# A 47-point DFT folded by the parity of its index, inside a fused FFT and feed-forward kernel

## The chip, the cores and the metric

The kernel runs on one core of a Trainium2 chip. Five engines matter: TensorE (PE in the profile; its weight loads are PEld), VectorE (DVE), ScalarE (ACT), GpSimd (POOL) and SyncE (SP), which issues most of the DMAs. The metric is the time of one execution on the device in microseconds (us), the median of the runs.

## The reference

The real part of a 2-D Fourier transform over 3008 positions and 256 features, for 8 batches, followed by a two-layer feed-forward block with a piecewise activation. Everything is float32.

```
X = np.fft.fft(x, axis=1)          # x: (8, 3008, 256)
X = np.fft.fft(X, axis=2)
x = X.real.reshape(B * S, D)
h = x @ w_in                       # w_in: (256, 2048)
g = np.where(h >= 1, h, np.where(h <= -1, 0.0, (h + 1) ** 2 / 4))
return g @ w_out                   # w_out: (2048, 256)
```

## The kernel before, in words

The 3008 positions are written as 64 x 47 (two coprime factors), so that their transform is a 47-point DFT followed by a 64-point DFT without twiddle factors. The transform over the 256 features is folded into `w_in` when the program starts (`fold_w_in`). Since the input is real, position s and position -s share most of the work: the kernel works on 24 of the 47 frequencies and on the sum and the difference of two halves.

**The transform of a batch** is a list of pieces (`fft_pieces`, L321). Stage 1 (`stage1`, L258) is the 47-point DFT. The host has already laid out x as two summands for each value; `fold_x` (L126) lets GpSimd add them: `y = t[:, 0] + t[:, 1]` (L131), 96 partitions by 512 elements, where the 96 partitions are two groups of 47 points and a padding row each. Then four float32 matmuls per tile (L270) take 128 columns of y as the stationary operand, and move the 96 columns of the constant `bm`, which holds two blocks of cosine and sine. Eight tiles (`XC`) make a batch: 32 matmuls of 94 used rows by 96 columns. Tile 0 also has the Nyquist feature: GpSimd subtracts 96 x 64 elements (L137, tile `yd`), and one small matmul (L275) transforms it. ScalarE copies the results out of PSUM into z, four copies of 64 x 192 a tile (L280) and two of 64 x 24 for the Nyquist feature (L283). `nyquist` (L285) and six pieces of stage 2 (`stage2`, L299, the 64-point DFT, matmul L309 with 128 columns moving) end the transform; ScalarE and VectorE split its result into a high and a low part, `pqh` and `pql`. In batch 0 the even tiles are not added on GpSimd: TensorE accumulates the two summands instead, which takes two matmuls for one.

**The feed-forward block** runs in units: one unit is one of 16 slices of 128 hidden features on one of three column chunks (482, 512 and 512 wide) of a batch, 48 units to a batch; batch 0 goes over its chunks twice with 8 slices each. `gemm1` (L350) makes two PSUM banks `uv` with six matmuls (L359). VectorE makes `us` (L362) and two halves of `h` (L364, L365); ScalarE computes the activation's square (L372, L373); VectorE finishes h (L374, two tiles of SBUF in, one out); ScalarE rounds it to `gh` (L375); GpSimd makes the rest `gl = h - gh` in two halves (L378). `gemm2` (L381) comes four units later (`LAG`): twelve matmuls (L402) that accumulate into four PSUM banks `acc`. The `uv` banks rotate over three buffers, `h` and `a` over three, `gh` and `gl` over four.

**The order.** Each engine runs its own instructions in a fixed order. A scheduler decides that order from the program text, except on TensorE for the first matmul of each piece of a later batch (`pinned`, L316) and for the start. The pieces of the next batch's transform are spread over the 48 units of the current batch (for batch 1: over units 25 to 47 of batch 0). The x tiles of the next batch come by SyncE into buffers tagged `xt`, four of them, which the weights' raw data shared while they were converted during batch 0; y rotates over three buffers. The loads of the first four x tiles are written at the first unit of the batch before (`FIRST_LOAD`, unit 21, for batch 1), the rest follow piece by piece.

Of the kernel before, what the change touches and what calls it, by code (L numbers as in the profile page):

```python
# [31 lines left out]
C_ORDER = [*range(1, 8), 0, *range(8, NC)]  # L32
WIDTH = [7 * NA + 34, CH, CH]

G_ORDER = np.arange(P).reshape(XC, GPC, 2, 2).transpose(0, 3, 1, 2).reshape(-1)


def _constants():
    a, b, k = (np.arange(n) for n in (NA, NBB, D))
    bm = np.zeros((P, 96))  # L40
    ang = 2 * np.pi * (np.outer(b, C_ORDER) % NBB) / NBB
    for t in range(2):
        o = t * 2 * NC
        bm[o : o + NBB, o : o + NC] = np.cos(ang)
        bm[o : o + NBB, o + NC : o + 2 * NC] = np.sin(ang)
# [22 lines left out]
START = "p0 p1 c0 p2 p3 c1 f0 p4 p5 p6 p7 d0 p8 p9 p10 c4 c5"  # L70
# [39 lines left out]
def fft_ffn_kernel(ctx: ExitStack, tc: tile.TileContext, x, cst, w_in, w_out, out):  # L110
# [7 lines left out]
    xt, yt, zt, nyb, pq = {}, {}, {}, {}, {}  # L118

    def load_x(b, q):  # L120
        tag, bufs = ("xt", 4) if b or q < 4 else ("gl", 4) if q < 7 else ("o", 2)
        t = sb.tile([96, 2, CH], F32, tag=tag, name=f"x_{b}_{q}", bufs=bufs)
        nc.sync.dma_start(t, x[b, q])
        xt[b, q] = t

    def fold_x(b, q):  # L126

        t = xt.pop((b, q))
        if b or q % 2:
            y = sb.tile([96, CH], F32, tag="y", name=f"y_{b}_{q}", bufs=3)  # L130
            nc.gpsimd.tensor_tensor(y, t[:, 0], t[:, 1], op=ALU.add)  # L131
            yt[b, q] = [y]
        else:
            yt[b, q] = [t[:, 0], t[:, 1]]
        if q == 0:
            y = sb.tile([96, NA], F32, tag="yd", name=f"yd_{b}", bufs=1)
            nc.gpsimd.tensor_tensor(y, t[:, 0, :NA], t[:, 1, :NA], op=ALU.subtract)  # L137
            yt[b, "d"] = y
# [39 lines left out]
    def load_w(n):  # L178
        if n >= len(jobs):
            return  # L180
        kind, *at = jobs[n]
# [8 lines left out]
        raws[n] = raw  # L190

    def convert_w(n):

        raw = raws.pop(n)
        low, high = raw[:, :, 0], raw[:, :, 1]
        if n in CV:
            tag, bufs = CV[n]
            t = sb.tile([P, 2, CH], U32, tag=tag, name=f"cv_{n}", bufs=bufs)
            man, exp = t[:, 0], t[:, 1]
            lowf, shifted = low.bitcast(F32), exp  # L200
        else:
# [54 lines left out]
        nc.scalar.activation(delta[:, f4 * 4 : f4 * 4 + 4], pt, AF.Copy)  # L256

    def stage1(b, q):  # L258
        for p in range(q, min(q + 2, XC)):
# [4 lines left out]
        z, y = zt[b], yt[b, q]
        bank = fft_bank(b, f"s1_{b}_{q}")
        pt = bank[:, : GPC * 96].rearrange("p (i n) -> p i n", i=GPC)
        for i in range(GPC):
            for j, part in enumerate(y):
                lhs = part[:, i * P : (i + 1) * P]
                mm = nc.tensor.matmul(pt[:, i], lhs, bm[:96, :], start=(j == 0), stop=(j == len(y) - 1))  # L270
                if i == 0:
                    pinned(b, mm)
        if q == 0:
            pd = bank[:NA, GPC * 96 : GPC * 96 + 2 * NC]
            nc.tensor.matmul(pd, yt[b, "d"], bm[:96, : 2 * NC], start=True, stop=True)  # L275
        for h in range(2):
            for m in range(2):
                src = pt[h * NA : (h + 1) * NA].rearrange("p i (t m c) -> p m c (i t)", t=2, m=2)[:, m]
                dst = z[m * NA : (m + 1) * NA, :, (2 * q + h) * 8 : (2 * q + h + 1) * 8]
                nc.scalar.activation(dst, src, AF.Copy)  # L280
        if q == 0:
            for m in range(2):
                nc.scalar.activation(z[m * NA : (m + 1) * NA, :, P], pd[:, m * NC : (m + 1) * NC], AF.Copy)  # L283
# [248 lines left out]
```

## Time and profile before

| What | Value |
|---|---|
| Median of 3 runs | 1766.23 us (1762.65 to 1767.64) |
| The profiled execution: its span, first to last instruction | 1761.8 us |
| The profiled execution: its own time beside the span | not given; the median of the runs lies 4.4 us above the span |
| Granted TensorE clock, mean | 0.997 |
| Stage-1 and Nyquist matmuls of stage 1 (L270, L275), instructions | 544 and 16 |
| GpSimd: gl (L378), y (L131), yd (L137), instructions | 765, 60, 8 |

The span is cut into engines' busy time; a busy share near 100% says that an engine has no rest, not that it runs at its peak, since matmuls overlap. What an engine waits for is listed with the engine and line that ended the wait. A float32 matmul (L270, L275, L287, L309, L246) shows as two instructions, a matmul of type float32r (L359, L402) as one.

### The profile page before, as it was taken

The page shows a single profiled execution, that of the slowest core. Times are in us where ns is not written, and L with a number is a line of the kernel's source. Part 1 is how long each engine was busy: PE and PEld are TensorE (multiplying, and loading weights), DVE is VectorE, ACT ScalarE, POOL GpSimd, SP SyncE. Part 2 cuts the span into 40 slices and gives each one's busy share as a digit, 9 for nine tenths or more (in the row PEclk, how much of TensorE's full clock was granted, in tenths as well). Part 3 has the DMA queues.
Part 4 walks back from the last instruction along what each step waited for, and adds up shares of the span by engine and source line. Part 5 has one row for each costly group of instructions (what it writes and reads, how often), then busy time and mean ns, then how long its engine had stood idle before and what let it go on. Part 6 is the DMA issues. An engine that isn't in the chain of part 4 may idle for free.

```text
span 1761.8 us, 21916 instructions
## 1 busy us (share of the span) xinstructions
PE 1734.5 (98%) x7982; PEld 1419.5 (81%) x7982; DVE 1428.0 (81%) x1745; ACT 1356.3 (77%) x1601; POOL 1203.4 (68%) x838
## 2 busy tenths in 40 slices
PE   9889999999999999999999999999999999999998
PEld 6766888888888888888888888888888888888777
DVE  6998788888887888778887788878888778888887
ACT  5777877877777877877778877788778787777776
POOL 1545966876668766787667876677676766667775
PEclk9999999999999999999999999999999999999999
DMA  7013331011010100111001100011000001000000
GB/s 230 12 65 102 101 107 57 28 50 42 1 51 28 53 30 1 51 50 31 30 10 51 50 28 24 23 39 51 26 24 34 1 23 35 8 25 6 17 24 24
DMA packets 29963, 72.51 MB, mean 41 GB/s; under 512 B 2976, under 2 KB 8224, under 8 KB 29856
## 3 DMA queue, kind: packets, MB, share of 16 engines
q1 hardware_dynamic: 29568, 70.08, 12.3%
q8 instruction: 62, 1.02, 0.3%
q10 hardware_dynamic: 288, 1.05, 0.2%
q14 instruction: 45, 0.37, 0.1%
HBM read 43.31 MB, written 27.81 MB: 40 GB/s over the span
## 4 chain that ended last, share of the span: by engine, by line
PE 73%; ACT 7%; POOL 5%; DVE 3%; issue 3%; ACTq 0%; POOLq 0%; DVEq 0%
PE acc L402 45%; PE uv L359 23%; POOL gl L378 5%; DVE h L374 3%; ACT gh L375 2%; PE s L270 2%; ACT a L373 2%; PE s L309 2%; ACT a L372 2%; ACT z L280 0%; ACT o L413 0%; DVE h L364 0%; DVE h L365 0%; POOL y L131 0%; DVE o L410 0%
## 5 line engine op out<-in xcount | busy, mean ns | idle before, releaser
L378 POOL TENSOR_TENSOR gl<-h,gh 128x512 fp32r<-128x512 f32 (+1 forms) x765 | 1096.7, 1456 | 510.6 <-ACT gh L375 478.0
L374 DVE SCALAR_TENSOR_TENSOR h<-a,h 128x1024 f32<-128x1024 f32 (+1 forms) x385 | 578.1, 1502 | 223.8 <-ACT a L373 222.2
L375 ACT ACTIVATE gh<-h 128x1024 fp32r<-128x1024 f32 (+1 forms) x385 | 400.6, 1041 | 346.1 <-DVE h L374 300.0
L402 PE MATMUL acc<-gl,woh 128*128 128x512 f32 (+1 forms) x1536 | 604.5, 394 | 9.2 <-POOL gl L378 9.2
L402 PE MATMUL acc<-gh,woh 128*128 128x512 f32 (+1 forms) x1536 | 608.0, 396 | 5.6 <-ACT gh L375 3.1
L402 PE MATMUL acc<-gh,wol 128*128 128x512 f32 (+1 forms) x1536 | 595.7, 388 | 0.0
L372 ACT ACTIVATE a<-h,biases 128x1024 f32<-128x1024 f32 (+1 forms) x385 | 431.8, 1122 | 9.7 <-DVE h L365 7.7
L373 ACT ACTIVATE a<-a 128x1024 f32<-128x1024 f32 (+1 forms) x385 | 398.7, 1036 | 7.1
L402 PEld LDWEIGHTS acc<-gl,woh 128*128 128x128 f32 x1536 | 288.6, 188 | 76.7 <-POOL gl L378 16.9
L402 PEld LDWEIGHTS acc<-gh,woh 128*128 128x128 f32 x1536 | 289.3, 188 | 66.3 <-ACT gh L375 4.9
L402 PEld LDWEIGHTS acc<-gh,wol 128*128 128x128 f32 x1536 | 289.5, 188 | 59.4
L364 DVE TENSOR_TENSOR h<-us,uv 128x512 f32<-128x512 f32 (+1 forms) x384 | 259.2, 675 | 67.2 <-POOL gl L378 26.0
L359 PE MATMUL uv<-pqh,wh 128*128 128x512 f32 (+1 forms) x768 | 303.8, 396 | 3.8 <-DVE us L362 3.3
L359 PE MATMUL uv<-pql,wh 128*128 128x512 f32 (+1 forms) x768 | 301.5, 393 | 0.0
L359 PE MATMUL uv<-pqh,wl 128*128 128x512 f32 (+1 forms) x768 | 299.1, 389 | 0.0
L362 DVE SCALAR_TENSOR_TENSOR us<-nyb,delta,uv 128x512 f32<-128x512 f32 (+1 forms) x384 | 278.4, 725 | 17.3 <-PE uv L359 16.9
L365 DVE TENSOR_TENSOR h<-us,uv 128x512 f32<-128x512 f32 (+1 forms) x384 | 255.9, 666 | 0.0
L359 PEld LDWEIGHTS uv<-pqh,wh 128*128 128x128 f32 x768 | 144.2, 188 | 42.7 <-DVE us L362 8.2
L359 PEld LDWEIGHTS uv<-pql,wh 128*128 128x128 f32 x768 | 144.5, 188 | 31.9
L359 PEld LDWEIGHTS uv<-pqh,wl 128*128 128x128 f32 x768 | 144.3, 188 | 30.3 <-issue 0.2
L131 POOL TENSOR_TENSOR y<-x 96x512 f32<-96x512 f32 x60 | 106.4, 1774 | 19.9 <-DMA x<-in_x_dram 8.1
L280 ACT ACTIVATE z<-s 64x192 f32<-64x192 f32 x256 | 86.8, 339 | 7.2 <-PE s L275 2.2
(54 smaller groups left out, 543.1 us busy)
## 6 DMA issues: line engine op xcount, KB each, us to landing
x<-in_x_dram SPq DMA_DIRECT2D x64, 384.0 KB, 3.4
out_dram<-o SPq DMA_DIRECT2D x30, 512.0 KB, 2.8
out_dram<-o SPq DMA_DIRECT2D x16, 482.0 KB, 3.2
nyb<-nyr SPq DMA_DIRECT2D x24, 256.0 KB, 3.2
raw<-in_moe_w_out_dram SPq DMA_DIRECT2D x8, 512.0 KB, 10.8
raw<-in_moe_w_in_dram SPq DMA_DIRECT2D x6, 512.0 KB, 4.5
part<-o SPq DMA_DIRECT2D x4, 512.0 KB, 3.3
o<-part SPq DMA_DIRECT2D x4, 512.0 KB
```

The source lines that it names most:

```text
L131: nc.gpsimd.tensor_tensor(y, t[:, 0], t[:, 1], op=ALU.add)
L280: nc.scalar.activation(dst, src, AF.Copy)
L359: nc.tensor.matmul(t[:, :n], w[m][:, cols], r[:, m, :n], start=(j == 0), stop=(j == 2))
L362: nc.vector.scalar_tensor_tensor(us, nyb[b, k][:, :n], delta[:, f : f + 1], uv[0], op0=ALU.mult, op1=ALU.add)
L364: nc.vector.tensor_tensor(h[:, 0], us, uv[1], op=ALU.subtract)
L365: nc.vector.tensor_tensor(h[:, 1], us, uv[1], op=ALU.add)
L372: nc.scalar.activation(a[:, sl], h[:, sl], AF.Relu, bias=half, scale=0.5)
L373: nc.scalar.activation(a[:, sl], a[:, sl], AF.Square)
L374: nc.vector.scalar_tensor_tensor(h[:, sl], a[:, sl], 1.0, h[:, sl], op0=ALU.min, op1=ALU.max)
L375: nc.scalar.activation(gh[:, sl], h[:, sl], AF.Copy)
L378: eng.tensor_tensor(gl[:, sg], h[:, sg], gh[:, sg].bitcast(F32), op=ALU.subtract)
L402: nc.tensor.matmul(acc[:, :n], w[:, f, wc], g[:, sg], start=(first and j == 0), stop=(last and j == 2))
```

## The change

The points b and 47 - b of the 47-point DFT have the same cosine and opposite sines. The new code adds and subtracts them first, so that 24 rows instead of 47 stand for one group, once for the cosine part and once for the sine part. A row block of 24 (`HB`) fits five times into 120 rows (`KR`, five groups, `GJ`), where two groups of 47 fitted into 94.

- The host lays out x as [120 partitions, 2, 4, 128]: four summands for each value (the two of before, each at b and at 47 - b). Six full tiles and a half one (7, `XC`) make a batch. The Nyquist feature sits in a slot of the half tile, and its own matmul and copies are gone.
- `fold_x` adds summand 1 to 0 and 3 to 2, in place, in one GpSimd instruction of 120 x 4 x 128 (for the half tile 96 x 2 x 128, and a subtraction of 24 x 2 x 64).
- `mirror_x`, for batches 1 to 7, makes the sum and the difference of the two results, in place, in two GpSimd instructions of 120 x 2 x 128 (120 x 128 for the half tile).
- `stage1` has 26 matmuls a batch, 120 rows by 120 columns: four a full tile, two for the half one. In batch 0 there is no mirror: 26 matmuls of 240 columns, two accumulated for each result.
- ScalarE copies 64 x 240 elements, four times a full tile, and 64 x 120 and 64 x 96, twice each, for the half one.
- x rotates over five buffers of `xt`; the three y buffers and `yd` are gone. The first four x loads of a batch are written four units (`LOAD_AHEAD`) ahead of the first unit in which that batch's transform may run, its first fold two units and its first mirror one unit ahead. `stage1` folds up to two tiles ahead and mirrors one ahead.
- The constants loaded first grow from 226 to 490 columns.

The core of the diff:

```diff
-XC = 8
-GPC = 4
+HB = 24
+GJ = 5
+KR = GJ * HB
+XC = 7
...
-        t = xt.pop((b, q))
-        if b or q % 2:
-            y = sb.tile([96, CH], F32, tag="y", name=f"y_{b}_{q}", bufs=3)
-            nc.gpsimd.tensor_tensor(y, t[:, 0], t[:, 1], op=ALU.add)
-            yt[b, q] = [y]
...
+        pair = t.rearrange("p r (k two) x -> p two (r k) x", two=2)
+        n = KR if q < XC - 1 else KR - HB
+        nc.gpsimd.tensor_tensor(pair[:n, 0], pair[:n, 0], pair[:n, 1], op=ALU.add)
+        if n < KR:
+            nyq = pair[n:, :, :, :NA]
+            nc.gpsimd.tensor_tensor(nyq[:, 0], nyq[:, 0], nyq[:, 1], op=ALU.subtract)
+
+    def mirror_x(b, q):
...
+            nc.gpsimd.tensor_tensor(t[:, :, 1], t[:, :, 0], t[:, :, 2], op=ALU.add)
+            nc.gpsimd.tensor_tensor(t[:, :, 3], t[:, :, 0], t[:, :, 2], op=ALU.subtract)
...
-        for p in range(q, min(q + 2, XC)):
-            if (b, p) in xt and (b, p) not in yt:
+        for p in range(q, min(q + 3, XC)):
+            if (b, p) in xt:
                 fold_x(b, p)
+                if p < q + 2:
+                    mirror_x(b, p)
...
-        for i in range(GPC):
-            for j, part in enumerate(y):
-                lhs = part[:, i * P : (i + 1) * P]
-                mm = nc.tensor.matmul(pt[:, i], lhs, bm[:96, :], start=(j == 0), stop=(j == len(y) - 1))
...
+        for r in range(n):
+            if b:
+                for m in range(2):
+                    mm = nc.tensor.matmul(pt[:, m, r], t[:, r, 2 * m + 1], bm[:KR, m], start=True, stop=True)
...
+            else:
+                for k in range(2):
+                    nc.tensor.matmul(
+                        pt[:, :, r], t[:, r, 2 * k], bm[:KR, : 2 + k : 1 + k], start=(k == 0), stop=(k == 1)
+                    )
...
-            if r == (0 if b else FIRST_LOAD) and b + 1 < NB:
-                for q in range(4):
-                    load_x(b + 1, q)
+            for nb in range(1, NB):
+                ahead = (per * (nb - 1) if nb > 1 else FIRST_DFT) - i
+                if ahead == LOAD_AHEAD:
+                    for q in range(4):
+                        load_x(nb, q)
+                elif ahead == 2:
+                    fold_x(nb, 0)
+                elif ahead == 1:
+                    mirror_x(nb, 0)
```

What this does to the order is seen best on GpSimd, around unit 103. In the names the first number behind `gl` is the unit, the first two behind `x` and `y` are batch and tile. Before:

```order
L378 TENSOR_TENSOR gl_102_4492<-h_102_4487,gh_102_4491 128x482 x2
L378 TENSOR_TENSOR gl_103_4539<-h_103_4534,gh_103_4538 128x482 x2
L131 TENSOR_TENSOR y_3_6_4876<-x_3_6_4510 96x512
L378 TENSOR_TENSOR gl_104_4573<-h_104_4568,gh_104_4572 128x482 x2
L378 TENSOR_TENSOR gl_105_4607<-h_105_4602,gh_105_4606 128x482 x2
L378 TENSOR_TENSOR gl_106_4654<-h_106_4649,gh_106_4653 128x482 x2
L378 TENSOR_TENSOR gl_107_4688<-h_107_4683,gh_107_4687 128x482 x2
L131 TENSOR_TENSOR y_3_7_5031<-x_3_7_4625 96x512
```

and the same place in the changed program:

```order
L405 TENSOR_TENSOR gl_102_4433<-h_102_4428,gh_102_4432 128x482 x2
L148 TENSOR_TENSOR x_4_0_5844<-x_4_0_5844 120x4x128
L158 TENSOR_TENSOR x_4_0_5844<-x_4_0_5844 120x2x128
L159 TENSOR_TENSOR x_4_0_5844<-x_4_0_5844 120x2x128
L405 TENSOR_TENSOR gl_103_4467<-h_103_4462,gh_103_4466 128x482 x2
L405 TENSOR_TENSOR gl_104_4515<-h_104_4510,gh_104_4514 128x482 x2
L405 TENSOR_TENSOR gl_105_4549<-h_105_4544,gh_105_4548 128x482 x2
L405 TENSOR_TENSOR gl_106_4583<-h_106_4578,gh_106_4582 128x482 x2
L148 TENSOR_TENSOR x_4_1_5846<-x_4_1_5846 120x4x128
L158 TENSOR_TENSOR x_4_1_5846<-x_4_1_5846 120x2x128
L159 TENSOR_TENSOR x_4_1_5846<-x_4_1_5846 120x2x128
L405 TENSOR_TENSOR gl_107_4617<-h_107_4612,gh_107_4616 128x482 x2
```

Where one instruction stood between two units, three now stand together. In a later batch's stretch such bursts stand behind the `gl` of units 95, 98, 102, 106, 109, 113 and 115 (of the 48 units 96 to 143, and so on in each batch); before, the eight y stood behind units 94, 98, 100, 103, 107, 110, 114 and 117.

TensorE meets the first tile of batch 4 in unit 144, long after that. Before:

```order
L359 MATMUL uv_144_1_6069<-pql_3_0_5340,wh1_70 128x482
L270 MATMUL s1_4_0_6094<-cs_66,y_4_0_6087 128x96 x4
L275 MATMUL s1_4_0_6094<-cs_66,yd_4_6089 64x48
L402 MATMUL acc_128_0_5651<-gh_140_5928,woh_73 128x512
L402 MATMUL acc_128_0_5651<-gh_140_5928,wol_74 128x512
```

and now:

```order
L386 MATMUL uv_144_1_6002<-pql_3_0_5168,wh1_70 128x482
L295 MATMUL s1_4_0_6025<-cs_66,x_4_0_5844 128x120 x4
L429 MATMUL acc_128_0_5581<-gh_140_5866,woh_73 128x512
L429 MATMUL acc_128_0_5581<-gh_140_5866,wol_74 128x512
```

The place of the piece is the same; its four matmuls are 120 columns wide, and the Nyquist matmul behind them is gone. Tile 0 of batch 4 is folded and mirrored some 37 units before TensorE reads it.

More of the change, by code (lines that the diff above doesn't have):

```diff
@@ L33, with _slots @@
 WIDTH = [7 * NA + 34, CH, CH]
-G_ORDER = np.arange(P).reshape(XC, GPC, 2, 2).transpose(0, 3, 1, 2).reshape(-1)
+def _slots():
+    table = np.full((XC, 2, 2, GJ), -1)
+    g = np.arange(120).reshape(XC - 1, 2, 2, GJ)
+    table[: XC - 1] = g.transpose(0, 2, 1, 3)
+    table[XC - 1, 0, 1, :4] = np.arange(120, 124)
+    table[XC - 1, 0, 0, :4] = np.arange(124, 128)
+    table[XC - 1, 0, 0, 4] = 0
+    return table
 def _constants():
-    a, b, k = (np.arange(n) for n in (NA, NBB, D))
-    bm = np.zeros((P, 96))
+    a, b, k = (np.arange(n) for n in (NA, HB, D))
+    bm = np.zeros((P, 3, KR))
     ang = 2 * np.pi * (np.outer(b, C_ORDER) % NBB) / NBB
[L42 to L45, printed above, removed]
+    for j in range(GJ):
+        o = slice(j * HB, (j + 1) * HB)
+        bm[o, 0, o] = np.cos(ang)
+        bm[o, 1, o] = np.sin(ang)
+        bm[o, 2, o] = -np.sin(ang)
+    bm = bm.reshape(P, 3 * KR)
     ang = 2 * np.pi * (np.outer(a, a) % NA) / NA
@@ L73 @@
     0: "o2",
-    1: "f1 d1 o3 p11",
-    2: "p12",
-    3: "p13 p14 l8 l9",
+    1: "f1 d1 o3 p10",
+    2: "p11",
+    3: "p12 p13 l8 l9",
     4: "c6",
@@ L92 @@
 }
-FIRST_LOAD, FIRST_DFT = 21, 25
+FIRST_DFT, LOAD_AHEAD = 25, 4
 N_EARLY = 8
@@ L116, in fft_ffn_kernel @@
     ps = ctx.enter_context(tc.tile_pool(name="ps", bufs=1, space=bass.MemoryType.PSUM))
-    xt, yt, zt, nyb, pq = {}, {}, {}, {}, {}
+    xt, zt, nyb, pq = {}, {}, {}, {}
+    folded, mirrored = set(), set()
     def load_x(b, q):
-        tag, bufs = ("xt", 4) if b or q < 4 else ("gl", 4) if q < 7 else ("o", 2)
-        t = sb.tile([96, 2, CH], F32, tag=tag, name=f"x_{b}_{q}", bufs=bufs)
-        nc.sync.dma_start(t, x[b, q])
+        tag, bufs = ("xt", 5) if b or q < 4 else ("gl", 4)
+        n = 2 if q < XC - 1 else 1
+        t = sb.tile([KR, 2, 4, P], F32, tag=tag, name=f"x_{b}_{q}", bufs=bufs)[:, :n]
+        nc.sync.dma_start(t, x[b, q, :, :n])
         xt[b, q] = t
     def fold_x(b, q):
-        t = xt.pop((b, q))
-        if b or q % 2:
-            y = sb.tile([96, CH], F32, tag="y", name=f"y_{b}_{q}", bufs=3)
-            nc.gpsimd.tensor_tensor(y, t[:, 0], t[:, 1], op=ALU.add)
-            yt[b, q] = [y]
[L133 to L138, printed above, removed]
+        t = xt[b, q]
+        if (b, q) in folded:
+            return
+        folded.add((b, q))
+        pair = t.rearrange("p r (k two) x -> p two (r k) x", two=2)
[5 more added lines that the diff above has]
+    def mirror_x(b, q):
+        t = xt[b, q]
+        if b and (b, q) not in mirrored:
+            mirrored.add((b, q))
+            nc.gpsimd.tensor_tensor(t[:, :, 1], t[:, :, 0], t[:, :, 2], op=ALU.add)
+            nc.gpsimd.tensor_tensor(t[:, :, 3], t[:, :, 0], t[:, :, 2], op=ALU.subtract)
     cs = wts.tile([P, _OFF[3]], F32, name="cs")
@@ L142, in fft_ffn_kernel @@
     bm, rm, odd = (cs[:, _OFF[i] : _OFF[i + 1]] for i in range(3))
-    cm = sb.tile([P, _OFF[7] - _OFF[3]], F32, tag="y", name="cm", bufs=3)
+    bm = bm.rearrange("p (m x) -> p m x", m=3)
+    cm = sb.tile([P, _OFF[7] - _OFF[3]], F32, tag="nyb", name="cm", bufs=4)
     mats = [[cm[:, (2 * m + h) * P : (2 * m + h + 1) * P] for h in range(2)] for m in range(2)]
@@ L181, in load_w @@
         kind, *at = jobs[n]
-        raw = sb.tile([P, CH, 2], U32, tag="xt" if n >= N_EARLY else RAW[n], name=f"raw_{n}", bufs=4)
+        raw = sb.tile([P, CH, 2], U32, tag="xt" if n >= N_EARLY else RAW[n], name=f"raw_{n}", bufs=5 if n >= N_EARLY else 4)
         if kind == "in":
@@ L202, in convert_w @@
             if n % 2 == 0:
-                f32s["pair"] = sb.tile([P, 2, CH], U32, tag="xt", name=f"cv_{n}", bufs=4)
+                f32s["pair"] = sb.tile([P, 2, CH], U32, tag="xt", name=f"cv_{n}", bufs=5)
             man, exp = f32s["pair"][:, n % 2], high
@@ L267, in stage1 @@
-        for i in range(GPC):
-            for j, part in enumerate(y):
-                lhs = part[:, i * P : (i + 1) * P]
[L270 to L275, printed above, removed]
+        pt = bank[:, : 2 * n * KR].rearrange("p (m r x) -> p m r x", m=2, r=n)
@@ L276, in stage1 @@
+        for r in range(n):
+            if b:
+                for m in range(2):
+                    mm = nc.tensor.matmul(pt[:, m, r], t[:, r, 2 * m + 1], bm[:KR, m], start=True, stop=True)
+                    if r + m == 0:
+                        pinned(b, mm)
+            else:
[3 more added lines that the diff above has]
+                    )
         for h in range(2):
+            cols = n * GJ
+            first = 20 * q + cols * h
+            if n == 1:
+                cols, first = (4, 120) if h else (5, 124)
@@ L277, in stage1 @@
             for m in range(2):
[L278 to L283, printed above, removed]
+                src = pt[h * NA : (h + 1) * NA, m].rearrange("p r (j c) -> p c (r j)", j=GJ)[:, :, :cols]
@@ L285, in nyquist @@
+                nc.scalar.activation(z[m * NA : (m + 1) * NA, :, first : first + cols], src, AF.Copy)
     def nyquist(b):
@@ L323, in fft_pieces @@
         for q in range(XC):
-            pieces.append((4, lambda q=q: stage1(b, q)))
+            pieces.append((4 if q < XC - 1 else 2, lambda q=q: stage1(b, q)))
         pieces.append((2, lambda: nyquist(b)))
@@ L502 @@
     xs = np.stack([xs[:, n][..., g], xs[:, neg][..., np.where(g == 0, P, D - g)]])
-    xs = xs.reshape(2, NB, NA, NBB, XC, GPC, 2, 2).transpose(1, 4, 6, 3, 0, 5, 7, 2)
-    xp = np.zeros((NB, XC, 2, 2 * NC, 2, GPC, 2, NA), xs.dtype)
-    xp[:, :, :, :NBB] = xs
+    slots = _slots()
+    used = (slots >= 0)[:, :, :, :, None, None]
+    xp = np.zeros((NB, XC, GJ, HB, 2, 4, 2, NA), xs.dtype)
+    for k in range(4):
+        bs = np.arange(HB) if k < 2 else (NBB - np.arange(HB)) % NBB
+        part = np.where(used, xs[k % 2].transpose(0, 3, 2, 1)[:, slots][..., bs, :], 0)
+        if k >= 2:
+            part[..., 0, :] = 0
+        xp[:, :, :, :, :, k] = part.transpose(0, 1, 4, 5, 2, 3, 6)
     arrays = {
-        "x": xp.reshape(NB, XC, 96, 2, CH),
+        "x": xp.reshape(NB, XC, KR, 2, 4, P),
         "cst": _CONST,
```

13 lines of the change are left out of this document (6 added, 7 removed).

## The prediction

> **What bounds the kernel now.** First the head of the page, then the windows view from 205 to 1540 us (first row) and the waits of TensorE in the same stretch (the other two).
>
> ```profile
> span 1761.8 us, 21916 instructions
> PE 1734.5 (98%) x7982; PEld 1419.5 (81%) x7982; DVE 1428.0 (81%) x1745; ACT 1356.3 (77%) x1601; POOL 1203.4 (68%) x838
> ...
> 205.00:1540.00 1335.00, 1334.07 (x6211) 1105.45 (x6212) 1077.07 (x1280) 1045.90 (x1223) 953.54 (x659) 1.00 0.11 35
> ...
> PE s L270 <- ACT z L280: 1.1, 1, 1.1
> PE uv L359 <- DVE h L365: 0.4, 1, 0.4
> ```
>
> For 1335 us TensorE waits 1.5 us in all. A matmul taken away there shortens the kernel; work given to GpSimd (953.5 of 1335 us busy) costs nothing until it makes TensorE wait. Six of the seven later batches' transforms (batches 2 to 7) lie in that stretch, the seventh (batch 1) mostly ahead of it. I work against this execution's span, 1761.8 us; the median of the runs, 1766.2, is 4.4 us above it, and I add that at the end. A measurement of this kernel tells about 0.3% (5.3 us) from no change.
>
> **What TensorE saves.** The timeline of TensorE at three pieces of the transform: stage 1, stage 1 with the Nyquist row, stage 2. Columns are start, length, line, tiles; each f32 matmul shows as two instructions.
>
> ```profile
> 507.47 1.03 PE L270 MATMUL s<-cs,y 96*128 96x96 f32 x8
> 508.28 0.47 PE L402 MATMUL acc<-gh,woh 128*128 128x482 f32 x1
> 508.59 0.38 PE L402 MATMUL acc<-gh,wol 128*128 128x482 f32 x1
> 508.81 0.39 PE L402 MATMUL acc<-gl,woh 128*128 128x482 f32 x1
> ...
> 279.32 1.03 PE L270 MATMUL s<-cs,y 96*128 96x96 f32 x8
> 280.28 0.32 PE L275 MATMUL s<-cs,yd 96*64 96x48 f32 x2
> 280.52 0.51 PE L402 MATMUL acc<-gh,woh 128*128 128x512 f32 x1
> 280.87 0.40 PE L402 MATMUL acc<-gh,wol 128*128 128x512 f32 x1
> 281.10 0.40 PE L402 MATMUL acc<-gl,woh 128*128 128x512 f32 x1
> ...
> 264.38 1.05 PE L309 MATMUL s<-cs,z 128*128 128x128 f32 x8
> 265.18 0.48 PE L359 MATMUL uv<-pqh,wh 128*128 128x512 f32 x1
> 265.50 0.40 PE L359 MATMUL uv<-pqh,wl 128*128 128x512 f32 x1
> 265.73 0.40 PE L359 MATMUL uv<-pql,wh 128*128 128x512 f32 x1
> ```
>
> Lengths overlap, so I count from start to start. Stage 1: from 507.47 to the second matmul behind it, 508.59, is 1.12 us; one GEMM matmul (508.59 to 508.81) is 0.22; the piece costs 0.90 us, 0.112 an instruction. With the Nyquist pair: 1.55 - 0.23 = 1.32. Stage 2, with 128 columns moving and 128 rows: 1.12 - 0.23 = 0.89. So 96 and 128 columns, and 96 and 128 rows, have one price here, and I take 0.112 for 120 by 120 as well. A later batch costs 7 x 0.90 + 1.32 = 7.62 us in stage 1 now, and 26 x 2 x 0.112 = 5.82 then: **1.80 less, times seven is 12.6 us**.
>
> The Trainium skill, "TensorE: Matmul & The Clock Gate", step ③ of "Step-by-step", says that a matmul streams one moving column per cycle and that its time is purely the number of columns. By that 26 x 120 = 3120 columns would stand for 32 x 96 = 3072, and nothing would be saved; the rows above speak against it (0.90 for 96 columns, 0.89 for 128). The same page, "LDWEIGHTS", makes the load depend on the stationary operand's columns, not its rows; those stay 128, and the trace agrees.
>
> **What GpSimd gets.** The groups of GpSimd in 508.8 to 719.5 us, one batch, then L131 over the whole run (shortest, median, longest in ns).
>
> ```profile
> L378 POOL TENSOR_TENSOR gl<-h,gh 128x512 fp32r<-128x512 f32 x64 | 92.6, 1470 | 41.2 <-ACT gh L375 40.3
> L378 POOL TENSOR_TENSOR gl<-h,gh 128x482 fp32r<-128x482 f32 x32 | 44.4, 1409 | 15.1 <-ACT gh L375 13.3 <-PE uv L359 0.9 <-PE acc L402 0.4
> L131 POOL TENSOR_TENSOR y<-x 96x512 f32<-96x512 f32 x8 | 15.1, 1890 | 0.0
> L137 POOL TENSOR_TENSOR yd<-x 96x64 f32<-96x64 f32 x1 | 0.3, 317 | 3.4 <-DMA x<-in_x_dram 3.4
> ...
> L131 POOL TENSOR_TENSOR y<-x x60: 1265/1898/2297, 9.5 to 1396.3; 96x512 f32<-96x512 f32 x60
> ```
>
> A new fold has 512 elements a partition, as a y has: 1.27 us alone. A mirror has 256; between 64 elements (0.32) and 512 (1.27) in a straight line that is 0.72. A full tile is 1.27 + 2 x 0.72 = **2.7 us in one burst**, alone; by the mean of y (1.89, 1.49 times its shortest) 4.0. The half tile is 2.0 to 3.0. A batch takes 18 to 27 us where it now takes 15.4: GpSimd goes from 152 of 210.7 us (72%) to at most 164 (78%). The total fits. What counts is the burst: it stands ahead of the `gl` of a unit, and behind a late `gl` wait TensorE (`acc`) and VectorE (L364, whose `h` buffer `gl` must free).
>
> A hole of that size is in the trace already, on GpSimd (first five rows) and VectorE (the others):
>
> ```profile
> 510.99 1.29 POOL L131 TENSOR_TENSOR y<-x 96x512 f32<-96x512 f32 x1
> 515.64 0.32 POOL L137 TENSOR_TENSOR yd<-x 96x64 f32<-96x64 f32 x1 [3.36 <-DMA x<-in_x_dram]
> 515.92 4.78 POOL L378 TENSOR_TENSOR gl<-h,gh 128x482 fp32r<-128x482 f32 x4
> 520.67 2.22 POOL L131 TENSOR_TENSOR y<-x 96x512 f32<-96x512 f32 x1
> 522.92 2.42 POOL L378 TENSOR_TENSOR gl<-h,gh 128x482 fp32r<-128x482 f32 x2
> ...
> 513.86 1.15 DVE L374 SCALAR_TENSOR_TENSOR h<-a,h 128x964 f32<-128x964 f32 x1
> 518.36 0.66 DVE L364 TENSOR_TENSOR h<-us,uv 128x482 f32<-128x482 f32 x1 [1.60 <-POOL gl L378]
> 518.94 2.79 DVE L374 SCALAR_TENSOR_TENSOR h<-a,h 128x964 f32<-128x964 f32 x1
> ```
>
> From 510.99 to 515.92 GpSimd makes no `gl`, 4.9 us; VectorE then waits 1.60 us for it, L374 takes 2.79 where it took 1.15, another y of 2.22 us follows within 5 us, and TensorE waits for none of it (the two waits above are all it has). A burst of 2.7 to 4.0 us is shorter than this hole. Against it: the hole lies partly where no `gl` was due, and bursts come seven to a batch, every three or four units in their stretch. There GpSimd's spare time, (210.7 - 152.4 + 15.4)/48 = 1.5 us a unit, gives 5.4 us between bursts 3.5 units apart, so it catches up, with little over. Bounds for what TensorE waits: nothing, or the whole excess of a burst over a y, (4.0 - 1.9) x 7 x 7 = about 100 us. The hole is the nearer row; I take **3 us** in all.
>
> The slower L374 is the other side. It reads two tiles of SBUF, as y does, and 2.79 - 1.15 = 1.64 us of it goes while a y runs beside it. The Trainium skill, "GPSIMD Engine Reference", "Key points", says that GpSimd shares its SBUF interfaces with VectorE and contends with VectorE instructions of two SBUF inputs. By that rule the sum comes out as in the second rival below; the trace agrees with it in kind.
>
> **The rest.** The x loads of the next batch are issued earlier relative to the fold that needs them, and five buffers rotate instead of four; the wait for DMA in the hole (3.36 us here) should go, which the result of zero above prices at nothing. ScalarE's copies:
>
> ```profile
> L280 ACT ACTIVATE z<-s 64x192 f32<-64x192 f32 x256 | 86.8, 339 | 7.2 <-PE s L275 2.2 <-PE s L270 1.1
> L283 ACT ACTIVATE z<-s 64x24 f32<-64x24 f32 x16 | 3.3, 209 | 0.2
> ```
>
> By a line through these, 64x240 takes 376 ns and the last tile's four 274 on average: 24 x 0.376 + 4 x 0.274 = 10.1 us a batch against 32 x 0.339 + 2 x 0.209 = 11.3. ScalarE gains a little, off the path: nothing.
>
> Batch 0 must fold all seven tiles where it folded four, has a larger first constant load, and runs 26 matmuls of 240 columns (52 instructions) for 96 instructions and a Nyquist pair. The start of the run, GpSimd and TensorE:
>
> ```profile
> 7.23 0.32 POOL L137 TENSOR_TENSOR yd<-x 96x64 f32<-96x64 f32 x1 [5.97 <-DMA x<-in_x_dram]
> 18.77 1.27 POOL L131 TENSOR_TENSOR y<-x 96x512 f32<-96x512 f32 x1 [1.46 <-DMA x<-in_x_dram]
> ...
> 9.67 1.92 PE L270 MATMUL s<-cs,x 96*128 96x96 f32 x16
> 15.44 3.62 PE L246 MATMUL wps<-cv,cm 128*128 128x512 f32 x8
> 18.90 1.92 PE L270 MATMUL s<-cs,x 96*128 96x96 f32 x16
> ```
>
> The first x lands at 7.23 and TensorE starts on it at 9.67, so one fold of 1.27 fits between. Eight L246 of 512 columns take 18.90 - 15.44 = 3.46, 0.433 each; 240 columns 0.203; 52 of them 10.6 us against 96 x 0.112 + 0.4 = 11.2. Arrival paces the tiles up to 18.77. Bounds: 1 us gained, or each of three more folds late, 4 lost; I take **0.5**.
>
> Sum: 1761.8 - 12.6 + 3 + 0.5 = 1752.7; with 4.4, **1757 us**, 0.5% faster.
>
> **Rivals.** *The saving is given back.* If the bursts cost TensorE 0.25 us each, 49 of them are 12 us, and the time is 1766 (1761 to 1771 for 7 to 17 us). For it: the 1.60 us wait on VectorE, and the short rest between bursts. Against it: the hole. Chance 0.21.
>
> *GpSimd and VectorE's L374 become the bound where the bursts stand.* If the two exclude each other, as L374's loss beside a y suggests, a unit needs 2.42 us for its two `gl` and 1.15 for L374, both alone: 3.57 of the 4.39 us (210.7/48) that TensorE gives it. Twenty units leave 16.4 us; seven bursts alone need 6 x 2.7 + 2.0 = 18.2. It decides from the point where that rest is used up: 1.8 us short a batch, and more by the peaks of single bursts, 2 to 5 us in all, 14 to 35 for seven batches. With the rest of the sum (1761.8 - 12.6 + 0.5 + 4.4 = 1754.1) that is 1768 to 1789, say **1778**: slower. Against it: the y bursts already use 7.6 of those 16.4 us with no wait. Chance 0.18.
>
> *TensorE does not get shorter*, by the streaming rule above: moving columns set the time, 12.6 becomes about 0, and 1761.8 + 0.5 + 4.4 gives 1767. The equal prices of stages 1 and 2 speak against it. Chance 0.05.
>
> **How the numbers follow.** My forecast, bursts hidden, has 0.56, with 1750 to 1762 as its own range (waits 0 to 7, start -1 to 4, spread of a median 2); over nine tenths of it is faster than 1761. Low is its low end, 1750; high 1776 takes in the given-back case, the case of no shorter TensorE, and the near part of the second rival. Faster 0.52 (the forecast's nine tenths, and a little of the given-back case); same 0.29 (the rest of both, and no shorter TensorE); slower 0.19 (the second rival, and the far end of the given-back case).
>
> **What would show it.** Stage-1 pieces on TensorE still at 0.90 us for eight instructions, but 52 a batch; TensorE waits in the steady stretch staying below about 5 us; bursts of 2.7 to 4.0 us on GpSimd. It is wrong if TensorE waits for `gl` or for VectorE's `us` and `h` once per burst, or if the first 60 us grow by more than 4.

## The result, and the profile after

The changed kernel takes 1782.11 us (median of 4 runs, 1780.57 to 1784.24), the kernel before beside it 1765.28: ratio 1.0097, 95% interval 1.0082 to 1.0111. It is slower by 17 us where 9 us less were forecast, and it lies outside the range. The profiled execution spans 1782.5 us. One execution of the first spread, told below, took 1914.43 us at a granted clock of 0.843 and is left out of every number here.

First the head of the page after, the windows view from 215 to 1560 us (about the units that 205 to 1540 us held before), and the waits of TensorE in that stretch (us in total, times, longest).

```profile
span 1782.5 us, 21738 instructions
PE 1732.5 (97%) x7838; PEld 1407.3 (79%) x7838; DVE 1414.6 (79%) x1745; ACT 1351.0 (76%) x1553; POOL 1283.8 (72%) x932
...
215.00:1560.00 1345.00, 1329.67 (x6123) 1093.31 (x6122) 1062.09 (x1282) 1043.97 (x1189) 1018.32 (x735) 1.00 0.11 35
...
PE s L295 <- ACT z L310: 5.4, 6, 0.9
PE acc L429 <- DVE o L442: 3.4, 6, 0.6
PE uv L386 <- DVE h L392: 2.0, 4, 0.5
PE s L336 <- ACT nyt L317: 1.8, 5, 0.4
PE acc L429 <- ACT o L440: 1.4, 6, 0.2
PE ny L314 <- ACT z L310: 1.3, 1, 1.3
```

TensorE is idle for 1345.00 - 1329.67 = 15.3 us of the stretch, where it was idle for 0.9. No line names GpSimd: TensorE waits for PSUM banks that ScalarE and VectorE read out late. The work itself became shorter as forecast; the timeline of TensorE at a stage-1 piece of a later batch:

```profile
551.27 1.05 PE L295 MATMUL s<-cs,x 120*128 120x120 f32 x8
552.09 0.47 PE L429 MATMUL acc<-gh,woh 128*128 128x482 f32 x1
552.39 0.38 PE L429 MATMUL acc<-gh,wol 128*128 128x482 f32 x1
```

From 551.27 to 552.39 are 1.12 us, less 0.22 for one GEMM matmul: 0.90 for eight instructions of 120 by 120, as for 96 by 96, and 52 a batch instead of 64 and a Nyquist pair.

Where the time came from shows when units are followed. The table gives the start of a unit's first `uv` matmul, in us, read from the trace of each kernel; the last row is the mean of five batches, (unit 336 - unit 96) / 5. The columns beside "before" and "after" are experiments that are told below.

| Unit | before | after | no mirrors | four h | four h, no mirrors | four x only |
|---|---|---|---|---|---|---|
| 0 | 33.3 | 36.7 | 36.3 | 37.0 | 36.2 | 36.7 |
| 24 | 159.6 | 168.1 | 166.1 | 163.6 | 162.7 | 165.5 |
| 48 | 278.0 | 291.3 | 283.1 | 283.4 | 275.9 | 290.9 |
| 96 | 488.4 | 503.1 | 492.4 | 493.7 | 484.6 | 505.3 |
| 336 | 1544.6 | 1567.7 | 1537.9 | 1542.8 | 1532.4 | 1570.1 |
| 383 | 1741.5 | 1762.7 | 1732.9 | 1735.3 | 1725.4 | 1766.3 |
| a batch | 211.24 | 212.93 | 209.10 | 209.81 | 209.57 | 212.96 |

After loses 3.4 us before unit 0, 9.9 us more by unit 48, then 1.7 us a batch where it should gain 1.8; only the last batch, in which no transform runs beside it, is shorter. The windows view of units 0 to 24, after and in the first experiment below, in which that stretch of the program is the same (length, then busy time and instructions by engine; behind them the granted clock):

```profile
36.70:168.10 131.40, 117.19 (x494) 87.66 (x493) 120.20 (x175) 90.65 (x109) 63.78 (x49) 0.96 0.17 56
```

```profile
36.10:165.10 129.00, 115.07 (x495) 86.13 (x494) 119.55 (x175) 90.51 (x109) 63.72 (x49) 0.99 0.18 56
```

So some 2.4 us of the loss before unit 24 go with this one execution's clock, 0.96 against 0.99. The kernel before takes 126.3 us there, and the run with four h 126.6.

Now the waits of VectorE for `gl`, before and after:

```profile
DVE h L364 <- POOL gl L378: 26.0, 25, 2.4
```

```profile
DVE h L391 <- POOL gl L405: 60.2, 51, 4.1
```

and how one of them comes about; GpSimd (first five rows), then VectorE, in the timeline after:

```profile
528.00 0.74 POOL L148 TENSOR_TENSOR x<-x 96x256 f32<-96x256 f32 x1 [2.24 <-DMA x<-in_x_dram]
528.82 1.27 POOL L151 TENSOR_TENSOR x<-x 24x128 f32<-24x128 f32 x1
530.16 0.46 POOL L158 TENSOR_TENSOR x<-x 120x128 f32<-120x128 f32 x1
530.58 0.47 POOL L159 TENSOR_TENSOR x<-x 120x128 f32<-120x128 f32 x1
531.00 7.08 POOL L405 TENSOR_TENSOR gl<-h,gh 128x482 fp32r<-128x482 f32 x5
...
530.82 0.71 DVE L389 SCALAR_TENSOR_TENSOR us<-nyb,delta,uv 128x482 f32<-128x482 f32 x1
533.47 0.66 DVE L391 TENSOR_TENSOR h<-us,uv 128x482 f32<-128x482 f32 x1 [1.94 <-POOL gl L405]
```

GpSimd makes no `gl` for 5.2 us, 2.24 of them waiting for tile 6 and the rest folding and mirroring it. VectorE is ready for the next unit's `h` at 531.5, but needs the buffer of three units before, whose `gl` is late: L391 starts at 533.47. From then on VectorE runs late, and with its order fixed everything behind L391 does: the `uv` banks' release, the copies of `o`, and by way of h ScalarE's copies too. This timeline makes that path plausible; what shows it is the run with a fourth buffer for h, below.

### The profile page after: what moved, and what is told of

It reads as the page before. It is cut to its first block, busy times and chain, and to the rows that moved or that the text cites. A ratio compares the mean times of both kernels' runs of the same rounds, so it can differ in the third digit from the quotient of the medians.

```text
span 1782.5 us, 21738 instructions
## 1 busy us (share of the span) xinstructions
PE 1732.5 (97%) x7838; PEld 1407.3 (79%) x7838; DVE 1414.6 (79%) x1745; ACT 1351.0 (76%) x1553; POOL 1283.8 (72%) x932
## 4 chain that ended last, share of the span: by engine, by line
PE 67%; ACT 13%; POOL 7%; issue 6%; DVE 5%; DMA 2%; SPq 0%; ACTq 0%; POOLq 0%; DVEq 0%
PE acc L429 42%; PE uv L386 20%; POOL gl L405 6%; DVE h L401 4%; ACT gh L402 4%; ACT a L400 4%; ACT a L399 3%; PE s L336 2%; ACT z L310 2%; PE s L295 2%; DMA x<-in_x_dram 1%; DMA raw<-in_moe_w_out_dram 1%; POOL x L148 1%; POOL x L159 1%; DVE h L392 0%
## 5 line engine op out<-in xcount | busy, mean ns | idle before, releaser
L405 POOL TENSOR_TENSOR gl<-h,gh 128x512 fp32r<-128x512 f32 (+1 forms) x765 | 1117.6, 1485 | 455.1 <-ACT gh L402 428.4
L401 DVE SCALAR_TENSOR_TENSOR h<-a,h 128x1024 f32<-128x1024 f32 (+1 forms) x385 | 566.5, 1472 | 221.5 <-ACT a L400 220.7
L391 DVE TENSOR_TENSOR h<-us,uv 128x512 f32<-128x512 f32 (+1 forms) x384 | 259.3, 675 | 96.4 <-POOL gl L405 60.2
L148 POOL TENSOR_TENSOR x<-x 120x512 f32<-120x512 f32 (+1 forms) x56 | 86.6, 1547 | 32.6 <-DMA x<-in_x_dram 28.3
L310 ACT ACTIVATE z<-s 64x240 f32<-64x240 f32 (+1 forms) x224 | 81.8, 365 | 10.2 <-PE s L300 4.8
## 6 DMA issues: line engine op xcount, KB each, us to landing
raw<-in_moe_w_out_dram SPq DMA_DIRECT2D x8, 512.0 KB, 11.6
```

What stands on the lines that cost most here:

```text
L148: nc.gpsimd.tensor_tensor(pair[:n, 0], pair[:n, 0], pair[:n, 1], op=ALU.add)
L310: nc.scalar.activation(z[m * NA : (m + 1) * NA, :, first : first + cols], src, AF.Copy)
L391: nc.vector.tensor_tensor(h[:, 0], us, uv[1], op=ALU.subtract)
L401: nc.vector.scalar_tensor_tensor(h[:, sl], a[:, sl], 1.0, h[:, sl], op0=ALU.min, op1=ALU.max)
L405: eng.tensor_tensor(gl[:, sg], h[:, sg], gh[:, sg].bitcast(F32), op=ALU.subtract)
```

## The experiments

The first theory (T1) went by TensorE's largest wait. The half tile's piece of four instructions should cost 0.45 us and costs 2.44, in six of six batches. The timeline after at the first of TensorE's three waits there, and ScalarE's copy of tile 5 that it waits for:

```profile
592.40 0.70 PE L295 MATMUL s<-cs,x 120*128 120x120 f32 x4 [0.91 <-ACT z L310]
593.67 0.50 PE L429 MATMUL acc<-gh,woh 128*128 128x512 f32 x1 [0.57 <-DVE o L442]
...
591.57 0.77 ACT L310 ACTIVATE z<-s 64x240 f32<-64x240 f32 x2
```

The piece stands at the change of accumulators (unit 20), two units behind tile 5, and both share the one bank `fft`. Rivals: GpSimd's mirrors are what makes everything late (T2); the loss is one of the start and of batch 1 (T3).

**Another place for the half tile.**

```diff
-            pieces.append((4 if q < XC - 1 else 2, lambda q=q: stage1(b, q)))
+            pieces.append((5 if q < XC - 1 else 2, lambda q=q: stage1(b, q)))
```

> Only the pace of the transform's pieces is changed: a full stage-1 piece counts 5 instead of 4, so that tile 5 (a full one) comes at the change of accumulators in unit 20 and the half tile in unit 24. Theory T1 (the half tile at the change, two units behind tile 5, costs 2.44 us instead of about 0.45, six times): the cost goes, the half tile's piece falls to 0.45 to 0.6 us, TensorE's waits for z and for o at the change nearly vanish, and the time falls by 10 to 14 us to about 1770 us. Theory T2 (GpSimd's bursts make everything late, and where the pieces stand is no matter): 1780 to 1784 us, the cost turns up at another piece. Theory T3 (the loss lies in the first 50 units): less than 3 us.

Measured: 1796.74 us, ratio 1.0177 (1.0162 to 1.0192), slower than the change by another 14 us (the ratios' difference); a batch takes 215.17 us. The half tile's piece does fall to 0.45 us. TensorE's waits from 215 to 1570 us in this run:

```profile
PE uv L386 <- DVE h L392: 7.2, 13, 1.0
PE acc L429 <- ACT o L440: 7.0, 5, 1.6
PE acc L429 <- DVE o L442: 5.4, 6, 0.9
```

The cost turned up elsewhere, and larger, while VectorE still waits 60.7 us for `gl`. T1 took the place where TensorE pays for the cause, and falls.

**Mirrors left out, in batches 1 to 7 and in batch 1 alone.** The matmuls take the folded summands, so the sums and differences are missing from what is computed.

```diff
-        if b and (b, q) not in mirrored:
+        if False and (b, q) not in mirrored:
...
-                    mm = nc.tensor.matmul(pt[:, m, r], t[:, r, 2 * m + 1], bm[:KR, m], start=True, stop=True)
+                    mm = nc.tensor.matmul(pt[:, m, r], t[:, r, 2 * m], bm[:KR, m], start=True, stop=True)
```

In the second run the first condition reads `b > 1`, and the operand is `t[:, r, 2 * m + (b > 1)]`.

> The mirrors are left out in batches 1 to 7: the matmuls take the folded summands as they are, so the output lacks the sums and differences; TensorE, ScalarE and the transfers do the same work, GpSimd some 68 us less. T2 (bursts on GpSimd): the steady loss and that of the transition from batch 0 to batch 1 go, 1760 to 1766 us, with the half tile's piece below 1 us. T1 (placement): the half tile still costs about 2.4 us, only the transition gives something back, 1774 to 1780 us. T3 (half of the loss is the transition's bursts): about 5 us, 1777 us, nearly all of it between units 8 and 48.

> The mirrors are left out in batch 1 alone, whose transform stands in units 25 to 47; its output lacks them, all else is as in the change. T3: what GpSimd's bursts cost in the transition comes back, units 24 to 32 fall by 4 to 6 us, the time to about 1777 us, and the batches after it cost what they cost in the change. T1: 0 to 2 us. T2: the share of one batch in seven and the dense place, 5 to 8 us.

Measured: 1754.86 us (ratio 0.9934, 0.9915 to 0.9953) and 1776.41 us (1.0063, 1.0048 to 1.0078). So the mirrors cost 27.3 us, more than T2 expected, 5.7 of them in batch 1 and the rest in the six batches after it. A batch takes 209.10 us, 2.1 less than before, with the half tile still at the change of accumulators: there its piece costs 0.51 us (median of six). T2 holds; of T3 only batch 1's share.

**The start: constants behind tile 0.**

```diff
-    nc.sync.dma_start(cs, cst[:, : _OFF[3]])
...
-    run_steps(LOADS)
+    run_steps("x0")
+    nc.sync.dma_start(cs, cst[:, : _OFF[3]])
+    run_steps(LOADS[3:])
```

> The load of the first constants (now 490 columns, 0.25 MB) is issued behind that of tile 0 instead of ahead of it. If the start's 3.4 us come of the larger first transfer, ahead of which no fold can begin, the first fold starts about 1.3 us earlier (7.7 instead of 9.05 us) and unit 0 by about 1 to 1.5 us (35.4 instead of 36.7); the time falls by 1 us, which the runs hardly resolve, but the trace shows. If the folds themselves (one for each tile instead of every second, 1.27 us each) hold TensorE, unit 0 moves by less than 0.5 us.

The first fold in the timeline after, and in this run:

```profile
9.05 1.26 POOL L148 TENSOR_TENSOR x<-x 120x512 f32<-120x512 f32 x1 [7.79 <-DMA x<-in_x_dram]
```

```profile
6.38 1.28 POOL L148 TENSOR_TENSOR x<-x 120x512 f32<-120x512 f32 x1 [5.12 <-DMA x<-in_x_dram]
```

It starts 2.7 us earlier and unit 0 1.9 us earlier (34.8), more than half of the 3.4 us; the median, 1782.15 us (1.0090, 1.0074 to 1.0106), is that of the change. So 1.9 us hang on the first load's place ahead of tile 0; that its size is the reason is likely, but no run changes the size alone. Before unit 0 TensorE also waits for folds (L148), 3.4 us in four places after and 3.0 in three in this run; before the change it waits for none there. A gain of 1.9 us is smaller than the interval of the ratio, 0.0016 to either side or 2.8 us, so the runs can't tell whether it lasts.

**The same work on GpSimd, one instruction at a time.** In batches 2 to 7 each fold and each mirror is tied behind the `gl` of the unit before it.

```diff
+                if nb > 1 and 0 <= X_AHEAD - ahead < 3 * XC:
+                    if ahead == X_AHEAD:
+                        x_ops[nb] = ops_x(nb)
+                    next(x_ops[nb])()
```

`ops_x` yields the fold and the two mirrors of each tile in turn; `X_AHEAD` is 3.

> In batches 2 to 7 GpSimd does the same folds and mirrors, but one instruction of them between the gl of two units instead of three in a row; batch 1 is as in the change. Theory T2a (three in a row, 2.7 to 4.0 us, make gl late, VectorE's h waits for it, and evictions and uv banks come late with it; one of 0.74 to 1.3 us beside 2.5 to 3 us of gl fits into a unit of 4.4 us): most of the 21 us that the mirrors of batches 2 to 7 cost (27 less the 6 of batch 1) come back, 1758 to 1768 us, a batch takes 209 to 210 us instead of 213, the half tile's piece is below 0.8 us. Theory T2b (GpSimd's time costs wherever it stands, by sharing SBUF with VectorE): 1778 to 1784 us.

Measured: 1806.51 us (median of three runs; 1.0214, 1.0193 to 1.0234). Neither case expected this. TensorE and VectorE in the waits:

```profile
PE s L307 <- POOL x L163: 27.0, 13, 3.6
...
DVE h L403 <- POOL gl L417: 18.3, 16, 4.1
```

VectorE's waits fell as T2a says, but the mirrors (now L163) came too late for stage 1, which had not been foreseen: the first `gl` of a unit starts 2.1 to 3.6 units behind its `uv` in this run (units 96 to 335; 2.1 to 4.0 in the change), so three units of lead are next to none. The second try begins earlier.

```diff
-X_AHEAD = 3
+X_AHEAD = 8
...
-                if ahead == LOAD_AHEAD:
+                if ahead == (LOAD_AHEAD if nb == 1 else X_AHEAD + 4):
```

> The spread folds and mirrors again (one instruction between the gl of two units, batches 2 to 7, three h buffers), but begun 8 units ahead instead of 3, and the loads 12 ahead: in the first spread TensorE waited 27 us for mirrors that stood behind the gl of a unit, and gl runs three to four units behind the uv of its unit. If bursts are what delays gl beyond three h buffers, TensorE's waits for mirrors go and the time is 1758 to 1768 us, VectorE's waits for gl 15 to 25 us. If any GpSimd work delays gl too much, wherever it stands: 1775 us or more, with VectorE's waits for gl near 60 us.

Measured: 1771.59 us (1.0040, 1.0025 to 1.0055), VectorE's waits for `gl` 20.6 us. That is 10.5 us less than the change with GpSimd doing the same work; the expected 1758 to 1768 was missed, and a batch takes 211.23 us, as before the change. The loads come earlier too, and GpSimd's waits for x tiles in the steady stretch go from 13.5 us to none, so the run doesn't part the bursts from late loads. Late loads alone don't cost TensorE this much, however: with four h, below, GpSimd waits 19.0 us for x tiles in that stretch and the time is the best. The half tile's piece still costs 2.2 us here.

**Mirrors on VectorE.**

```diff
-            nc.gpsimd.tensor_tensor(t[:, :, 1], t[:, :, 0], t[:, :, 2], op=ALU.add)
-            nc.gpsimd.tensor_tensor(t[:, :, 3], t[:, :, 0], t[:, :, 2], op=ALU.subtract)
+            nc.vector.tensor_tensor(t[:, :, 1], t[:, :, 0], t[:, :, 2], op=ALU.add)
+            nc.vector.tensor_tensor(t[:, :, 3], t[:, :, 0], t[:, :, 2], op=ALU.subtract)
```

> The two mirrors of a tile are made by VectorE instead of GpSimd, everywhere. T2a and T2b alike: GpSimd is at its load of before (1195 us), VectorE gets about 92 instructions of 0.35 to 0.4 us, some 35 us on 1415: if only GpSimd's time is scarce, 1757 to 1766 us. If it is VectorE's lateness that costs, whatever causes it, 1766 to 1776 us. If neither is scarce and the loss has another cause, 1780 us or more.

Measured: 1841.44 us (1.0412, 1.0397 to 1.0428), the worst of all, at a mean granted clock of 0.979 in the profiled execution (0.995 in the change's). By its number that is the third case, but what that case says (another cause) doesn't follow, since the move made a wait of its own. VectorE's timeline at a place where TensorE waits, then the waits of VectorE and of TensorE in the whole run:

```profile
556.53 0.64 DVE L392 TENSOR_TENSOR h<-us,uv 128x482 f32<-128x482 f32 x1
558.41 1.42 DVE L158 TENSOR_TENSOR x<-x 120x256 f32<-120x256 f32 x1 [1.24 <-POOL x L148]
559.75 1.42 DVE L159 TENSOR_TENSOR x<-x 120x256 f32<-120x256 f32 x1
561.10 0.70 DVE L389 SCALAR_TENSOR_TENSOR us<-nyb,delta,uv 128x482 f32<-128x482 f32 x1
...
DVE x L158 <- POOL x L148: 69.3, 30, 4.2
PE uv L386 <- DVE us L389: 40.9, 17, 4.4
```

A mirror on VectorE stands ahead of `us` and waits there for GpSimd's fold, 69.3 us in all, and beside `gl` it takes 1.42 us. So this run doesn't tell whose lateness counted in the change; it shows a longer wait of the same sort.

**A fourth buffer for h, and its control.** The room is taken from x.

```diff
-        h = sb.tile([P, 2, CH], F32, tag="h", name=f"h_{i}", bufs=3)[:, :, :n]
+        h = sb.tile([P, 2, CH], F32, tag="h", name=f"h_{i}", bufs=4)[:, :, :n]
...
-        tag, bufs = ("xt", 5) if b or q < 4 else ("gl", 4)
+        tag, bufs = ("xt", 4) if b or q < 4 else ("gl", 4)
```

The control has the second edit alone (in both, the other uses of the two tags follow).

> h gets a fourth buffer, and x's buffers go from five to four, which makes room for it; the mirrors stay on GpSimd, three instructions in a row. If a late gl reaches TensorE through h's buffers (VectorE's first h of a unit waits until GpSimd has read the h of three units before), VectorE's 60 us of waits for gl fall below 20 us and the time to 1762 to 1772 us. If it reaches TensorE in another way (gl itself, or VectorE slowed by sharing), 1779 to 1785 us with those waits gone.

> The other half of the run with four h buffers by itself: x's buffers go from five to four, h keeps three. If the fourth h buffer brought the 27 us, this stays at 1780 to 1788 us (a load later by one piece can only cost), and VectorE's waits for gl stay at about 60 us. If the smaller number of x buffers brought it, by moving the folds and mirrors to later places, 1755 to 1765 us.

Measured: 1755.44 us (0.9927, 0.9913 to 0.9942) with four h buffers, the fastest kernel that computes everything and faster than expected; 1786.80 us (1.0125, 1.0110 to 1.0140) for the control. In the traces the order of the instructions is the same in both on all engines, so the difference, 31 us between the medians and 35 by the ratios, is the buffer's alone. In a steady batch it is 3.2 us (212.96 against 209.81), where the changed kernel lost 1.7 to the kernel before. The waits of VectorE for `gl`, and those of TensorE from 210 to 1545 us, with four h:

```profile
DVE h L391 <- POOL gl L405: 3.8, 1, 3.8
...
PE acc L429 <- DVE o L442: 2.5, 5, 0.6
PE acc L429 <- ACT o L440: 1.4, 6, 0.2
PE ny L314 <- ACT z L310: 0.2, 1, 0.2
```

against the control's

```profile
DVE h L391 <- POOL gl L405: 60.1, 47, 4.5
```

TensorE's waits fall to 4.1 us. What is left stands at the change of accumulators, where the half tile's piece still costs 0.5 to 1.7 us, 1.2 on average.

**What else the fourth buffer does.** First the kernel before with it (room from folding in place and from moving the start's constants), then the changed kernel with it and without mirrors in batches 1 to 7, whose sums and differences are missing again.

```diff
-            y = sb.tile([96, CH], F32, tag="y", name=f"y_{b}_{q}", bufs=3)
-            nc.gpsimd.tensor_tensor(y, t[:, 0], t[:, 1], op=ALU.add)
-            yt[b, q] = [y]
+            nc.gpsimd.tensor_tensor(t[:, 0], t[:, 0], t[:, 1], op=ALU.add)
+            yt[b, q] = [t[:, 0]]
...
-        h = sb.tile([P, 2, CH], F32, tag="h", name=f"h_{i}", bufs=3)[:, :, :n]
+        h = sb.tile([P, 2, CH], F32, tag="h", name=f"h_{i}", bufs=4)[:, :, :n]
```

> The kernel before with a fourth h buffer; room for it comes from folding in place (no y buffers) and from the start's constants in nyb's buffers. The kernel before has 26 us of the same waits of VectorE for gl. If these cost TensorE little there (its waits in the steady stretch are 1.5 us in all), 1763 to 1768 us, and the change's own worth beside equal buffers is 8 to 13 us. If the h buffers were short in both kernels, 1752 to 1760 us, and the change's worth beside equal buffers is near nothing.

> Four h buffers and four x buffers, and the mirrors left out in batches 1 to 7 (the output lacks the sums and differences). If the h buffers are the only way in which the mirrors reach TensorE, this equals the four h buffers with mirrors: 1752 to 1756 us. If the mirrors also cost by sharing SBUF with VectorE or by late gl, it is faster by 4 us or more, 1745 to 1751 us.

Measured: 1760.85 us (0.9980, 0.9970 to 0.9991) and 1747.56 us (0.9902, 0.9888 to 0.9917). The first lies between the two cases expected, the second in the case in which the mirrors cost by another way too. In the kernel before the buffer, with the edits that make room for it, is worth 4 us, none of it in the steady batches (211.25 against 211.24). Beside equal buffers the change is worth 0.9980 - 0.9927 = 0.0053 of the time, 9 us. With four h the mirrors still cost 0.9927 - 0.9902 = 0.0025, 4 us by the ratios, whose intervals are 0.0015 to either side, and 9.9 us between the two profiled executions: hardly anything in the steady batches (209.81 against 209.57), 7.5 us by unit 48, where batch 1's seven tiles stand close together.

So the h buffers aren't the only way from the mirrors to TensorE. From unit 24 to unit 48 the mirrors cost 6.6 us with four h (119.8 against 113.2) and 6.2 with three (123.2 against 117.0): the fourth buffer gives nothing back there. TensorE's waits for `gl` itself in this stretch, with four h and without the mirrors:

```profile
PE acc L429 <- POOL gl L405: 5.8, 5, 2.1
```

```profile
PE acc L429 <- POOL gl L405: 2.1, 4, 0.7
```

That is 3.7 of the 6.6 us.

**Four h buffers and the constants behind tile 0.**

Both edits together, as shown above.

> Four h buffers and four x buffers as in the run that did best, and the load of the first constants behind that of tile 0. In the change by itself this load order moved unit 0 from 36.7 to 34.8 us, and the time by nothing that the runs resolve. If with four h buffers nothing later takes the 1.9 us back, 1752 to 1754 us, ratio 0.9915 to 0.9925; if batch 1's folds and mirrors in units 24 to 47 set the end of the first batch, unit 48 stays at about 283 us and the ratio at 0.993.

Measured: 1755.71 us (0.9929, 0.9915 to 0.9942), the same as without the second edit. In the profiled executions unit 0 comes 1.8 us earlier than without it (35.2) and unit 383 1.3 us (1734.0), which the runs can't resolve.

## Why the prediction was wrong, step by step

- **TensorE saves 12.6 us: right.** The price of 0.112 us an instruction held, 52 a batch held. Without mirrors a batch is 2.14 us shorter than before, with four h 1.43 (1.80 forecast).
- **"The hole is the nearer row; I take 3 us": the step that failed.** The mirrors alone measure 27 us. The size of a burst was right (three instructions, 1.3 + 0.74 + 0.74 us at the median), and so was that TensorE doesn't wait for `gl` in the steady stretch. What was wrong was to take the hole's zero wait on TensorE as a measure of VectorE's slack. The way on was named, "VectorE (L364, whose `h` buffer `gl` must free)", but not priced: VectorE already waited 26.0 us there in 25 places, so at these places the three buffers were used up before the change. Over units 96 to 335 such waits grew from 13.1 us, at three units of a batch, to 35.4, at eight, with new ones behind the bursts; with four h they are 0.7. The late `h` beside the hole was made good without a wait of TensorE; those that the seven bursts of a batch make, within 20 units, were not. The control and the run with four h differ in this alone, and by 31 us.
- **What would have pointed to it** (an estimate made afterwards): the time that a buffer is held. From the start of L391 (L364 before) to the end of the same unit's second `gl`, paired in order of time over units 96 to 335, the traces have a median of 11.6 us before the change and 13.3 or more in one unit of ten; after, 13.6 in one of ten and 14.7 at most. Three buffers allow three units, 3 x 4.39 = 13.2 us: room for 1.6 us at the median, where a fold with two mirrors takes 2.8. Four allow 17.6, more than the longest with four h, 14.8.
- **The start at +0.5 us: mis-sized.** Unit 0 came 3.4 us later, within the bounds named; 1.9 of it go with the order of the first loads, a gain that the runs can't resolve in the time, and TensorE waits for the folds, as the bound of 4 us had it. Batch 1's mirrors in units 24 to 47, which the sum didn't treat apart, cost 5.7 us, and about as much with four h.
- **x loads and ScalarE at nothing:** GpSimd still waits for x tiles (2.24 us in the timeline above, 13.5 us in the steady stretch), so the wait that should go stayed, ahead of the longest gap in `gl` shown. With three h it lengthens a gap; with four h it is longer (19.0 us) and costs nothing that shows. ScalarE's copies show up in TensorE's waits, but as late, not as too long: the waits nearly vanish with the fourth h.
- **The rivals.** *GpSimd and L374 become the bound* named the right side and nearly the size (1778 for 1782), by another mechanism. If the two engines excluded each other for lack of time, a buffer would not help; L374 (now L401) has a median of 1468 ns after and of 1465 with four h. The working for it misread a row: it let all of L374's 1.64 us beyond 1.15 go beside a y, but that y started at 520.67 and L374 ended at 521.73, so the two ran together for 1.06 us. *The saving is given back* had the mechanism of waits at each burst, but too small. *TensorE does not get shorter* fell: the matmuls did get fewer at the same price.

The Trainium skill, "Perfetto Trace Analysis", "Optimization Strategy", says that the same gap repeating on the engine that should be saturated can mean that there is too little SBUF or PSUM for the next tile, and names the number of buffers. The 2.44 us at the half tile, six times of six, were such a gap, and the run with four h agrees in part: the piece falls to 1.2 us on average, by a buffer of a tile that TensorE never touches.

Not settled: why the half tile still costs 2.2 us when the folds and mirrors are spread, though VectorE's waits for `gl` over units 96 to 335 are only 5.9 us there (13.1 before the change); why it costs 1.2 with four h; and whether an earlier start shortens the run.

## What to carry to other kernels

Before giving an off-path engine a burst, look for waits that already end on it, on any engine: a wait that costs TensorE nothing now (26 us on VectorE here) says that the buffers between the two are used up at that place, and a longer burst can then reach TensorE under the names of other engines. Price a burst against the depth of the rotation that it holds, not against the engine's free share; and where a stall repeats, test the buffer count before the place of the piece that stalls. With the buffer, the change is a gain of 0.7% over the kernel before, or of 0.5% over the kernel before with the same buffer; without it, a loss of 1%.

## What the runs showed of the hardware

- A float32 matmul of 120 rows by 120 columns costs what one of 96 by 96 does: 0.112 us for each of its two instructions.
- A two-input GpSimd operation on 120 partitions took at the shortest 0.46 us for 128 elements, 0.72 for 256 and 1.26 for 512; the last took 2.28 at the longest.
- A VectorE operation with two SBUF inputs, 120x256, took 0.41 us while GpSimd did nothing and 1.42 us beside `gl` (above). The former, in the run with mirrors on VectorE:

```profile
188.59 0.41 DVE L158 TENSOR_TENSOR x<-x 120x256 f32<-120x256 f32 x1
```
